# Computing the output of nine of 32 heads with 512-column matmuls and a DRAM scratch, in a decode attention kernel with gradients

## Chip, cores, metric

The kernel runs on one core of a Trainium2 chip. The metric is device time in microseconds, lower is better. Every run named here was in the fast state. A ratio between two kernels is the mean time of one's fast runs over the mean of the other's fast runs of the same rounds, so it is not quite the ratio of the medians that are quoted beside it. In the profile PE is TensorE's matmul side and PEld its weight loads, DVE is VectorE, ACT ScalarE, POOL GpSimd, and SPq the queue of SyncE, which issues the transfers. L205 is a line of the kernel of that run. Where a figure comes from the records of a trace and not from a view of the profile, the text says so.

## The reference

One query row per head, 32 heads, 8192 keys, head dimension 128, bf16. It returns the attention output and its gradients with respect to q, k and v.

```python
def _fwd_reference(q, k, v):
    scale = q.shape[-1] ** -0.5
    scores = jnp.einsum('bhqd,bhkd->bhqk', q, k) * scale
    attn = _softmax(scores, axis=-1)
    return jnp.einsum('bhqk,bhkd->bhqd', attn, v)
# reference: out, vjp = jax.vjp(_fwd_reference, q, k, v); returns out and vjp(grad_out)
```

Per head: p = softmax(q.K scale), o = p.V, dp = V.do, ds = p (dp - sum(p dp)) scale, dq = ds.K, dK = outer(ds, q), dV = outer(p, do). K and V of a head are 2.1 MB each and are read once. dK and dV are as large and are written once.

## The kernel before

A head's V lies in SBUF as 128 rows of 64 slots of 128 values. V has two buffers, so the load for head h+2 waits until head h has let go. The output o comes from 64 matmuls, each with a whole 128x128 block of V as weights and a single moving column. The sum of p dp is found as do.o, with one more matmul.

```python
    def contract(Xt, rep, out_col, first=0, last=NT):
        for n in range(first, last):
            nc.tensor.matmul(out_col, lhsT=Xt[:, n, :], rhs=rep[:, n, 0:1],
                             start=(n == 0), stop=(n == NT - 1), skip_group_check=True)
    # ... cut ...
    for h in range(H + 1):
        p_ = h - 1
        if h < H:
            x = st[h] = {}
            rows_bc(h)                 # q and do rows to all partitions, into the bank x["s"]
            for u in range(NCH):
                k_blocks(h, u)         # VectorE transposes of K, four a head
            k_scores(h)                # PE: scores
        if h > 0:
            ds_of(p_)                  # needs sum(p dp) in x["m"][:, 1:2]
            outer(p_, "dk", 0)
            dq_of(p_, 0)
        # ... cut: softmax, more of dk and dq, K load ...
        v_copy(h, 0)
        v_transposes(h, 1)
        v_transposes(h, 2)
        contract(Vt[h], x["p"], x["m"][:, 2:3])
        nc.scalar.copy(o_all[:, h:h + 1], x["m"][:, 2:3])
        v_scores(h, 0)                 # PE: dp
        v_scores(h, 1)
        v_transposes(h, 3)
        nc.tensor.matmul(x["m"][:, 1:2], lhsT=do_f[:, h:h + 1].to_broadcast([P, P]), rhs=o_all[:, h:h + 1],
                         start=True, stop=True, skip_group_check=True)
        v_scores(h, 2)
        v_scores(h, 3)
        outer(h, "dv", 0)              # VectorE; the fourth one issues the store of dv
        outer(h, "dv", 1)
        outer(h, "dv", 2)
        if 0 < h and h + 2 < H:
            load_v(h + 2)
        outer(h, "dv", 3)
```

## Time and profile before

| | before |
|---|---|
| time, median of 3 | 645.52 us (645.49 to 646.38) |
| profiled span, mean granted TensorE clock | 644.6 us, 0.601 |
| busy: PE, DVE, ACT | 482.0, 505.9, 180.7 us |
| HBM bytes | 134.23 MB read, 134.23 MB written |

The page's own lines are shown in the prediction. One plain head in order of time is needed as well, because the change inserts work there. The columns are start, length, engine, line, operation, tiles, count, and in brackets what an idle engine had waited for.

```profile
317.68 0.51 ACT L309 ACTIVATE p_rep<-e,rinv 128x256 bf16<-128x256 f32 x1 [1.98 <-DVE rinv L307]
320.07 4.63 DVE L215 TENSOR_TENSOR G_dv<-p_rep,qd 128x2048 bf16<-128x2048 bf16 x4 [2.13 <-DMA out_dram<-G_dv]
320.90 1.82 PE L205 MATMUL m_ps<-p_rep,Vt 128*128 128x1 bf16 x64
...
324.49 0.34 SPq L78 DMA_DIRECT2D Vt<-in_v_dram  x1
324.84 4.62 DVE L146 STREAM_TRANSPOSE XK_sb<-Kt 128x1024 f32<-128x1024 f32 x4
...
325.62 0.58 PE L200 MATMUL dp_ps<-do_blk,XT_sb 128*128 128x2 bf16 x16 [0.64 <-ACT XT_sb L179]
```

p is ready at 318.19. DVE does not start dv until 320.07, because the buffer of dv is still being stored. The 64 one-column matmuls take 1.82 us in all. dp is complete at 326.20, and at 328.30 three of the four K transpositions are done.

### The profile page before, as it was taken

The page shows a single profiled execution, that of the slowest core. Times are in us where ns is not written, and L with a number is a line of the kernel's source. Part 1 is how long each engine was busy: PE and PEld are TensorE (multiplying, and loading weights), DVE is VectorE, ACT ScalarE, POOL GpSimd, SP SyncE. Part 2 cuts the span into 40 slices and gives each one's busy share as a digit, 9 for nine tenths or more (in the row PEclk, how much of TensorE's full clock was granted, in tenths as well). Part 3 has the DMA queues.
Part 4 walks back from the last instruction along what each step waited for, and adds up shares of the span by engine and source line. Part 5 has one row for each costly group of instructions (what it writes and reads, how often), then busy time and mean ns, then how long its engine had stood idle before and what let it go on. Part 6 is the DMA issues. An engine that isn't in the chain of part 4 may idle for free.

```text
span 644.6 us, 20935 instructions
## 1 busy us (share of the span) xinstructions
PE 482.0 (75%) x9673; PEld 443.9 (69%) x9673; DVE 505.9 (78%) x653; ACT 180.7 (28%) x332; POOL 0.7 (0%) x6
## 2 busy tenths in 40 slices
PE   3998898886777877768776787677876777877780
PEld 2887788785676766768666687567776676866670
DVE  5999899767977679867788777787767986778761
ACT  2333333322233231333222332123322233231230
POOL 0000000000000000000000000000000000000000
PEclk9666666665566655666556665566665566655665
DMA  8999999999999999999999999999999999999985
GB/s 350 404 428 429 424 427 424 428 429 421 418 429 428 428 425 430 430 426 431 425 428 428 430 426 428 428 428 427 427 429 431 424 432 424 430 426 429 427 362 244
DMA packets 19718, 269.80 MB, mean 419 GB/s; under 512 B 2352, under 2 KB 2352, under 8 KB 2864
## 3 DMA queue, kind: packets, MB, share of 16 engines
q1 hardware_dynamic: 19584, 268.47, 98.2%
q8 instruction: 75, 1.23, 0.7%
q14 instruction: 11, 0.09, 0.0%
q10 hardware_dynamic: 48, 0.01, 0.0%
HBM read 134.23 MB, written 134.23 MB: 416 GB/s over the span
## 4 chain that ended last, share of the span: by engine, by line
DMA 62%; PE 24%; DVE 9%; ACT 1%; issue 1%; SPq 0%; DVEq 0%; ACTq 0%
DMA Vt<-in_v_dram 61%; PE T_ps L188 15%; DVE XK_sb L146 4%; DVE G_dv L215 4%; PE m_ps L205 3%; PE dp_ps L200 2%; PE s_ps L157 2%; PE dp_ps L205 1%; DVE G_dk L215 1%; DMA Kt<-in_k_dram 1%; PE m_ps L300 1%; ACT p_rep L309 0%; PE s_ps L173 0%; ACT XT_sb L179 0%; PE m_ps L288 0%
## 5 line engine op out<-in xcount | busy, mean ns | idle before, releaser
L188 PE MATMUL T_ps<-ident_f,Vt 128*128 128x128 f32 x1024 | 217.0, 383 | 27.3 <-DMA Vt<-in_v_dram 24.7
L188 PEld LDWEIGHTS T_ps<-ident_f,Vt 128*128 128x128 f32 x1024 | 182.2, 206 | 45.2 <-PE m_ps L288 21.7
L215 DVE TENSOR_TENSOR G_dv<-p_rep,qd 128x2048 bf16<-128x2048 bf16 x128 | 148.2, 1220 | 60.9 <-DMA out_dram<-G_dv 52.8
L215 DVE TENSOR_TENSOR G_dk<-ds_rep,qd 128x2048 bf16<-128x2048 bf16 x128 | 155.6, 1218 | 4.6 <-DMA out_dram<-G_dk 3.6
L146 DVE STREAM_TRANSPOSE XK_sb<-Kt 128x1024 f32<-128x1024 f32 x128 | 148.3, 1214 | 5.8 <-DMA Kt<-in_k_dram 3.2
L179 ACT COPY XT_sb<-T_ps 128x1024 f32<-128x1024 f32 x128 | 128.7, 1008 | 83.9 <-PE T_ps L188 77.2
L157 PE MATMUL s_ps<-q_blk,XK_sb 128*128 128x4 bf16 x2048 | 59.8, 168 | 94.6 <-DVE pdt L239 87.6
L157 PEld LDWEIGHTS <-XK_sb 128*128 128x128 bf16 x2048 | 57.1, 104 | 103.9 <-DVE pdt L239 96.6
L200 PE MATMUL dp_ps<-do_blk,XT_sb 128*128 128x2 bf16 x2048 | 67.0, 164 | 18.0 <-ACT XT_sb L179 17.6
L200 PEld LDWEIGHTS <-XT_sb 128*128 128x128 bf16 x2048 | 65.5, 103 | 20.7 <-ACT XT_sb L179 20.2
L205 PE MATMUL dp_ps<-ds_rep,Kt 128*128 128x1 bf16 x2048 | 64.0, 165 | 0.4 <-DVE ds_rep L241 0.4
L205 PEld LDWEIGHTS <-Kt 128*128 128x128 bf16 x2048 | 59.5, 104 | 5.7 <-issue 5.6
L249 ACT COPY dq_all<-dp_ps 128x1 f32<-128x1 f32 x32 | 5.1, 159 | 205.2 <-PE dp_ps L205 182.8
L205 PEld LDWEIGHTS <-Vt 128*128 128x128 bf16 x2048 | 57.0, 96 | 0.7
L205 PE MATMUL m_ps<-p_rep,Vt 128*128 128x1 bf16 x2048 | 56.5, 163 | 0.0
L309 ACT ACTIVATE p_rep<-e,rinv 128x256 bf16<-128x256 f32 x32 | 16.3, 508 | 64.6 <-DVE rinv L307 64.6
L307 DVE RECIPROCAL rinv<-m_ps 128x1 f32<-128x1 f32 x32 | 5.4, 168 | 35.2 <-PE m_ps L300 35.1
L234 ACT CAST qd<-s_ps 128x256 bf16<-128x256 f32 x32 | 11.9, 372 | 32.5 <-PE s_ps L230 32.5
L299 ACT ACTIVATE e<-s_ps,nbias 128x64 f32<-128x64 f32 x32 | 10.1, 314 | 32.5 <-DVE nbias L295 32.5
L241 DVE SCALAR_TENSOR_TENSOR ds_rep<-dp_ps,pdt,p_s 128x256 bf16<-128x256 f32 x32 | 15.5, 484 | 4.6 <-PE dp_ps L200 1.3
L163 DVE TENSOR_TENSOR sm<-s_ps,in_quad 128x256 f32<-128x256 f32 x32 | 13.6, 425 | 6.0 <-PE s_ps L157 2.0
L300 PEld LDWEIGHTS m_ps<-rs,ones_f 128*128 128x128 f32 x64 | 17.6, 334 | 0.0
(44 smaller groups left out, 153.1 us busy)
## 6 DMA issues: line engine op xcount, KB each, us to landing
Vt<-in_v_dram SPq DMA_DIRECT2D x32, 2048.0 KB, 30.1
Kt<-in_k_dram SPq DMA_DIRECT2D x31, 2048.0 KB, 30.3
out_dram<-G_dv SPq DMA_DIRECT2D x30, 2048.0 KB, 34.5
out_dram<-G_dk SPq DMA_DIRECT2D x30, 2048.0 KB, 33.7
out_dram<-G_dv SPq DMA_DIRECT2D x4, 1024.0 KB, 14.4
out_dram<-G_dk SPq DMA_DIRECT2D x4, 1024.0 KB, 13.2
Kt<-in_k_dram SPq DMA_DIRECT2D x4, 512.0 KB, 5.1
out_dram<-fin_sb SPq DMA_DIRECT2D x2, 8.0 KB, 12.8
```

Of the source, the lines that this page charges most:

```text
L146: nc.vector.transpose(XK[h][:, :, :, u, :], slots(Kt[h], u, NCH).rearrange("p g d -> p (g d)").bitcast(F32).rearrange("p (g w j) -> p g w ...
L157: nc.tensor.matmul(out[:, g, :], lhsT=cols[:, g, c // 2, c % 2], rhs=q_blk[:, h, c, :], start=(c == 0), stop=(c == 2 * NB - 1), skip_group ...
L163: nc.vector.tensor_tensor(x["sm"][:], x["s"][:, 0:NT].rearrange("p (a g) -> p a g", a=NQ).unsqueeze(2) .to_broadcast([P, NQ, NCH, CH]), in ...
L179: nc.scalar.copy(X[:], st[h].pop("T")[:])
L188: nc.tensor.transpose(T_ps[:, i, :], words[:, m * P:(m + 1) * P], ident_f[:])
L200: nc.tensor.matmul(st[h]["dp"][:, n:n + 2], lhsT=X[:, i, e2, :], rhs=do_blk[:, h, e2, :], start=(e2 == 0), stop=(e2 == 1), skip_group_chec ...
L205: nc.tensor.matmul(out_col, lhsT=Xt[:, n, :], rhs=rep[:, n, 0:1], start=(n == 0), stop=(n == NT - 1), skip_group_check=True)
L215: nc.vector.tensor_tensor(slots(G, r, 4).rearrange("p n (a b) -> p n a b", b=R), slots(rep, r, 4).unsqueeze(2).to_broadcast([P, Q, D // R, ...
L234: nc.scalar.copy(x["qd"][:].rearrange("p a d -> p (a d)"), x["s"][:, 256:512])
L241: nc.vector.scalar_tensor_tensor(out=x["ds"][:], in0=x["dp"][:, 0:NT].unsqueeze(2).to_broadcast([P, NT, R]), scalar=pdt[:], in1=x["p_s"][: ...
L300: nc.tensor.matmul(x["m"][:, 0:1], lhsT=ones_f[:], rhs=rs[:], start=True, stop=True, skip_group_check=True)
L309: nc.scalar.activation(x["p"][:], e[:].unsqueeze(2).to_broadcast([P, NT, R]), ACT.Copy, scale=rinv[:])
```

## The change

The intent is to spend fewer instructions on o. In nine heads (2, 5, ..., 26) four columns of p become the weights and 512 columns of V stream past them. That makes 16 matmuls in place of 64, and their result is a 4x512 array whose four diagonal 128-wide blocks sum to o. Taking a diagonal across partitions is done by a DRAM scratch: each wide head writes its array, and one strided read near the end fetches the blocks of all nine heads. As o of such a head is only known at the end, VectorE computes the sum of p dp directly, and a matmul with a matrix of ones spreads it.

```diff
+WIDE = tuple(range(2, 28, 3))
+    def o_wide(h, first, last):
+        x = st[h]
+        for g in range(first, last):
+            nc.tensor.matmul(x["s"][0:R, :], lhsT=x["p"][:, R * g:R * (g + 1), 0],
+                             rhs=Vt[h][:, R * g:R * (g + 1), :].rearrange("p n d -> p (n d)"),
+                             start=(g == 0), stop=(g == NT // R - 1), skip_group_check=True)
+        if last == NT // R:
+            four = small.tile([R, R * D], F32, tag="four", name="four")
+            nc.scalar.copy(four[:], x["s"][0:R, :])
+            nc.sync.dma_start(scratch[WIDE.index(h), 0:R * R * D].rearrange("(a c) -> a c", a=R), four[:])
+
+    def pd_of(h):
+        # ... cut: junk and pd tiles ...
+        nc.vector.tensor_tensor_reduce(out=junk[:], in0=x["p_s"][:], in1=x["dp"][:, 0:NT], scale=1.0,
+                                       scalar=0.0, op0=ALU.mult, op1=ALU.add, accum_out=pd[:])
+        nc.tensor.matmul(x["m"][:, 1:2], lhsT=ones_s[:], rhs=pd[:], start=True, stop=True, skip_group_check=True)
             for u in range(NCH):
+                if u == NCH - 1 and p_ in WIDE:
+                    pd_of(p_)
                 k_blocks(h, u)
         v_transposes(h, 1)
+        if h in WIDE:
+            o_wide(h, 0, 8)
         v_transposes(h, 2)
-        contract(Vt[h], x["p"], x["m"][:, 2:3])
-        nc.scalar.copy(o_all[:, h:h + 1], x["m"][:, 2:3])
+        if h in WIDE:
+            o_wide(h, 8, 16)
+        else:
+            contract(Vt[h], x["p"], x["m"][:, 2:3])
+            nc.scalar.copy(o_all[:, h:h + 1], x["m"][:, 2:3])
         # ... cut: the do.o matmul only if h not in WIDE ...
+        if h == WIDE[-1] + 3:
+            nc.sync.dma_start(blocks[:], scratch[:].rearrange("h (a c) -> h a c", a=R)[:, :, 0:D])
         if h == H - 1:
+            # ... cut: sum of the blocks, transpose, nine columns of o_all ...
             result(o_all, out_0)
```

More of the change, by code (lines that the diff above doesn't have):

```diff
@@ L54 @@
     small = ctx.enter_context(tc.tile_pool(name="small", bufs=2))
+    dram = ctx.enter_context(tc.tile_pool(name="scr", bufs=1, space=bass.MemoryType.DRAM))
     psT = ctx.enter_context(tc.tile_pool(name="psT", bufs=2, space=PSUM))
@@ L136, in do_columns @@
         nc.scalar.copy(do_f[:], tp[:, 2, 0:H])
+    ones_s = consts.tile([P, P], F32)
+    nc.vector.memset(ones_s[:], 1.0 / scale)
+    scratch = dram.tile([len(WIDE), R * (R + 1) * D], F32, name="scratch")
+    blocks = consts.tile([len(WIDE), R, D], F32)
     o_all = consts.tile([P, H], F32)
@@ L206, in contract @@
                              start=(n == 0), stop=(n == NT - 1), skip_group_check=True)
+    def o_wide(h, first, last):
[9 more added lines that the diff above has]
+    def pd_of(h):
+        x = st[h]
+        junk = small.tile([P, NT], F32, tag="junk")
+        pd = small.tile([P, 1], F32, tag="pd")
+        nc.vector.tensor_tensor_reduce(out=junk[:], in0=x["p_s"][:], in1=x["dp"][:, 0:NT], scale=1.0,
+                                       scalar=0.0, op0=ALU.mult, op1=ALU.add, accum_out=pd[:])
+        nc.tensor.matmul(x["m"][:, 1:2], lhsT=ones_s[:], rhs=pd[:], start=True, stop=True, skip_group_check=True)
     def outer(h, which, r):
@@ L319 @@
         v_transposes(h, 3)
-        nc.tensor.matmul(x["m"][:, 1:2], lhsT=do_f[:, h:h + 1].to_broadcast([P, P]), rhs=o_all[:, h:h + 1],
-                         start=True, stop=True, skip_group_check=True)
+        if h not in WIDE:
+            nc.tensor.matmul(x["m"][:, 1:2], lhsT=do_f[:, h:h + 1].to_broadcast([P, P]), rhs=o_all[:, h:h + 1],
+                             start=True, stop=True, skip_group_check=True)
         v_scores(h, 2)
@@ L331 @@
             load_v(2)
+        if h == WIDE[-1] + 3:
+            nc.sync.dma_start(blocks[:], scratch[:].rearrange("h (a c) -> h a c", a=R)[:, :, 0:D])
         if h == H - 1:
+            block_sum = consts.tile([len(WIDE), D], F32)
+            nc.vector.reduce_sum(block_sum[:], blocks[:].rearrange("h a d -> h d a"), axis=AX.X)
+            turned = psT.tile([P, CH // 2, P], F32, tag="T", name="turned")
+            nc.tensor.transpose(turned[:, 0, 0:len(WIDE)], block_sum[:], ident_f[0:len(WIDE), 0:len(WIDE)])
+            nc.scalar.copy(o_all[:, WIDE[0]:WIDE[-1] + 1:WIDE[1] - WIDE[0]], turned[:, 0, 0:len(WIDE)])
             result(o_all, out_0)
```

## The prediction

The text is as it was recorded, with cuts marked where it told of the hardware what no trace or run of this case shows. Cut from its sum are the terms for the 16 wide matmuls of a head: they came to 4.5 us, five at a granted clock of 0.50 ("cold" in what is left) and eleven at 1.00, with 3.5 us (all at 1.00) and 6.8 us (all at 0.50) as limits. Less the 1.77 us removed this makes the +2.7 us (+1.7 to +5.0). No such matmul is in the trace before, so these were my estimates and not shown; the trace after has since given 215 to 216 ns from start to start at 1.00 and up to 427 at 0.50, 3.5 and 6.8 us for sixteen. The forecast came to 646.0 us: nothing in the middle, about 0.5 us of transfers and tail on the 645.5. That a few engines may carry a scratch write was a guess too. In the records of the changed kernel each such write is four packets of 2 KB, with four completions 11 to 21 us after the issue (and a fifth record 0.4 us after it, before the packets), where a V load has sixteen completions.

> **What bounds the kernel now.** I read the page's slices first, because they say which resource never rests:
>
> ```profile
> PE   3998898886777877768776787677876777877780
> PEld 2887788785676766768666687567776676866670
> DVE  5999899767977679867788777787767986778761
> ...
> DMA  8999999999999999999999999999999999999985
> ```
>
> No compute engine is full in more than a few slices; the DMA row is at 9 in all but three slices, at both ends. The windows view (columns: stretch, length, busy time and instruction count of PE, PEld, DVE, ACT, POOL, then granted clock, DMA share, GB/s) sharpens this:
>
> ```profile
> 200.00:300.00 100.00, 75.34 (x1512) 69.19 (x1511) 78.63 (x100) 27.54 (x51) 0.00 (x0) 0.59 1.01 427
> 300.00:400.00 100.00, 76.67 (x1518) 70.73 (x1517) 79.41 (x101) 28.43 (x51) 0.00 (x0) 0.59 1.01 428
> ```
>
> The DMA share is 1.01 and the rate 427 to 428 GB/s from 40 to 600 us; PE and DVE rest a quarter and a fifth of the time. The bytes cannot shrink: 134.23 MB read and 134.23 MB written make 268.46 MB, and 268.46 MB / 427.5 GB/s = 628 us. The other 17 us are the start and the end (the last two slices move 362 and 244 GB/s).
>
> The chain of waits looks different at first:
>
> ```profile
> DMA 62%; PE 24%; DVE 9%; ACT 1%; issue 1%; SPq 0%; DVEq 0%; ACTq 0%
> DMA Vt<-in_v_dram 61%; PE T_ps L188 15%; DVE XK_sb L146 4%; DVE G_dv L215 4%; PE m_ps L205 3%; PE dp_ps L200 2%; PE s_ps L157 2%; PE dp_ps L205 1%; DVE G_dk L215 1%; DMA Kt<-in_k_dram 1%; PE m_ps L300 1%; ACT p_rep L309 0%; PE s_ps L173 0%;
> ```
>
> It alternates a V load with the PE work that frees that V buffer, so it would seem that a longer contraction on PE lengthens the chain. The chain in order of time shows why I don't believe this:
>
> ```profile
> 264.52 31.12 DMA Vt<-in_v_dram
> ...
> 304.93 29.59 DMA Vt<-in_v_dram
> ```
>
> A V load is 2.1 MB, 4.9 us of the full rate, yet takes 29.6 to 31.1 us from issue to landing: about 25 us of it is standing behind other transfers. And the load issued later (40.41 us after the other) landed 38.89 us after it: the late issue was taken out of the standing time. The issue list says the same of all four streams (30.1, 30.3, 34.5 and 33.7 us). A head's four 2.1 MB transfers are 8.39 MB, 19.6 us at 427.5 GB/s; the head period in the timeline is 19.4 to 20 us. **The bound is the shared transfer rate, behind a queue some six transfers deep.**
>
> [...]
>
> **The change part by part**, for each of nine wide heads (2, 5, ..., 26).
>
> ```profile
> L205 PE MATMUL m_ps<-p_rep,Vt 128*128 128x1 bf16 x2048 | 56.5, 163 | 0.0
> L320 PE MATMUL m_ps<-o_all,do_f 128*128 128x1 f32 x64 | 12.6, 266 | 0.0
> L316 ACT COPY o_all<-m_ps 128x1 f32<-128x1 f32 x32 | 5.1, 159 | 18.6 <-PE m_ps L205 18.6
> L311 DVE TENSOR_SCALAR p_s<-e,rinv 128x64 f32<-128x64 f32 x32 | 8.2, 255 | 3.4
> ```
>
> These rows are for all 32 heads. Removed: 64 one-column matmuls, busy 56.5/32 = 1.77 us (a 163 ns row, but pipelined); the o copy, 0.16 us; the fp32 product do.o, 12.6/32 = 0.4 us.
>
> Added on PE: 16 matmuls of 512 columns. [...] In the timeline of a plain head the clock is 0.50 until about 321.3 us, with p ready at 318.2 and the second group of transposes done at 319.1, then 1.00 until about 324.5. [...] So **PE gets longer, not shorter**: 3.5 to 6.8 minus 1.8, or +1.7 to +5.0 us per wide head, my choice +2.7; nine heads +15 to +45 us of 482 busy. Moving fewer instructions does not pay: the 64 small ones already stream at 28 ns each.
>
> On DVE: the product-and-sum of 128x64, about the 255 ns of the p_s row, nine times 2.3 us of 506. Its fp32 all-ones matmul replaces the do.o one, 0.4 us. On ACT: a 4x512 copy; from 256 columns in 372 ns and 1024 in 1008, (1008-372)/768 = 0.83 ns a column, 0.58 us, +0.4 us on an engine that is 28% busy.
>
> Transfers: nine writes of 8 KB and one read of 18 KB, 92 KB, 0.2 us at full rate; as each write has only four rows, a few engines may carry them, so allow 1 us. Each write stands in SP's order before the next V load, which waits for later PE work (fourth transpose group) anyway; it blocks nothing new. The read, at the end of head 29 (near 584 us), stands behind a store that takes some 34 us, so it should land near 618 to 620; its sum is wanted near 624. It and its transposition fit beside a 1.34 us DVE idle stretch there, before the last dk work.
>
> Where does the +2.7 us go? Two places. (a) V is freed later by it, so the V load, and the dv store behind it, are issued later; 25 us of standing time absorb that: no change of landing. (b) The new sum needs the last dp scores and stands on DVE before the fourth K transposition of the next head. In the plain head shown by the timeline the K transpositions start at 324.8, three end at 328.3, and dp is done at 326.2; with +2.3 to +2.7 us dp is done near 328.8, so DVE waits 0.5, works 0.3, and the scores start about 1 us late (4 us late if all matmuls are cold). But DVE has slack:
>
> ```profile
> DVE G_dv L215 <- DMA out_dram<-G_dv: 50.7, 23, 3.6
> ```
>
> From 100 to 600 us (25 heads) DVE waited 50.7 us for stores to leave, 2 us a head, 6 us per wide head with its two plain neighbours. That exceeds 1 to 4 us, so compute catches up before the queue is any thinner than some 20 us. Sum on the path: 0 in the middle, 0.2 to 1 us of transfers and tail. **646.0 us.**
>
> **The rivals.** (1) *The V chain is the bound*: each wide head then puts +2.7 (1.7 to 5.0) us into every second link of a chain of even heads (the V load of h+2 waits for h), so of nine wide heads the chain that ends last would carry four or five: about 4.5 x 2.7 = 12 us, 658 us, up to 668. For it: the chain view, 24% PE. Against: the shrinking load time and DMA share 1.01. (2) *Compute becomes the bound*: all matmuls cold and DVE's waits not recoverable, 9 x (1 to 4) = 9 to 36 us, 655 to 681. For it: DVE 78% busy, PE waits for DVE; against: the 2 us a head that DVE itself waits for stores. (3) *It gains*: the wide form is quicker or helps the clock. Even if PE gained 1.8 us per wide head, the transfers would still need 628 us plus the ends: nothing. (4) *The scratch disturbs*: the read lands late and holds DVE in head 31, or slow small transfers unbalance the engines; 1 to 5 us, 647 to 651. The margin of 4 us speaks against it.
>
> **Range and chances.** The executions before lie in 645.49 to 646.38. Below, only noise: 644.5. Above, rival 4 or a little of 2: 648.5. Faster by over 2% needs fewer bytes or a higher rate, 0.01. Slower by over 2% (above 658.4) needs rival 1 or 2 in full, 0.03. Within 2%, 0.96.
>
> **What would show it.** Right: DMA share still 1.01 and some 427 GB/s in the middle; the 16 wide matmuls of a head taking 3.5 to 6.8 us, PE busy near 482 + 24 = 506; V loads issued 2 to 5 us later in wide heads and their time to landing shorter by as much; DVE's wait for dv stores smaller than before; the small score matmuls after a wide head starting about 1 us late. Wrong: a DMA share below 1 in the heads after wide ones, V landing intervals above 40 us, or DVE waiting for the block read near the end.

## The result, and the profile after

| | before | after |
|---|---|---|
| time, median of 4 | 645.53 us (645.49 to 646.38) | 646.53 us (646.36 to 646.68) |
| ratio to before | | 1.0012, 95% interval 0.9995 to 1.003 |
| profiled span, granted clock | 644.6 us, 0.601 | 644.6 us, 0.648 |
| busy: PE, DVE, ACT | 482.0, 505.9, 180.7 us | 495.5, 508.7, 184.3 us |
| instructions | 20935 | 20121 |

The time is the same within the noise. In the page after, two rows of the slices and one row of the costliest groups answer to the rows shown before:

```profile
PE   3998888886777977788777788877787787877780
...
DMA  8999999999999999999999999999999999999995
...
L218 PE MATMUL s_ps<-Vt,p_rep 128*4 128x512 bf16 x144 | 36.4, 398 | 0.0
```

The groups with shapes kept apart show the parts that the page left out:

```profile
L223 ACT COPY four<-s_ps 4x512 f32<-4x512 f32 x9 | 5.2, 576 | 7.3 <-PE s_ps L218 7.3
...
L230 DVE CUSTOM_DVE_ANT_0 junk<-p_s,dp_ps 128x64 f32<-128x64 f32 x9 | 1.7, 190 | 2.3 <-PE dp_ps L206 2.3
...
L230 DVE DVE_READ_ACCUMULATOR2_ANT pd<- 128x1 f32 x9 | 0.7, 83 | 0.0
```

A wide head's 16 matmuls are busy 36.4/9 = 4.04 us, against 1.77 us for the 64 that they replace. Fewer instructions took longer. The mean of 398 ns in the row is the length of one matmul, which overlaps the next, not the spacing. From start to start the records show 215 to 216 ns where the granted clock was 1.00, and up to 427 ns where it was 0.50.

The windows view from 300 to 400 us (columns as in the prediction) shows the transfers exactly as full as before:

```profile
300.00:400.00 100.00, 77.42 (x1465) 67.46 (x1464) 79.82 (x104) 28.11 (x50) 0.00 (x0) 0.62 1.01 428
```

Now wide head 17 in order of time, the counterpart of the plain head above:

```profile
336.87 0.51 ACT L337 ACTIVATE p_rep<-e,rinv 128x256 bf16<-128x256 f32 x1 [2.18 <-DVE rinv L335]
...
338.16 1.89 PE L218 MATMUL s_ps<-Vt,p_rep 128*4 128x512 bf16 x8
339.37 4.63 DVE L241 TENSOR_TENSOR G_dv<-p_rep,qd 128x2048 bf16<-128x2048 bf16 x4 [2.24 <-ACT XT_sb L185]
...
341.01 1.89 PE L218 MATMUL s_ps<-Vt,p_rep 128*4 128x512 bf16 x8
...
344.18 3.50 DVE L152 STREAM_TRANSPOSE XK_sb<-Kt 128x1024 f32<-128x1024 f32 x3 [0.17 <-DMA Kt<-in_k_dram]
...
345.87 0.55 PE L206 MATMUL dp_ps<-do_blk,XT_sb 128*128 128x2 bf16 x16 [0.78 <-ACT XT_sb L185]
...
347.60 0.18 DVE L230 CUSTOM_DVE_ANT_0 junk<-p_s,dp_ps 128x64 f32<-128x64 f32 x1
```

From p ready to dp complete takes 346.42 - 337.38 = 9.0 us here, against 326.20 - 318.19 = 8.0 us in the plain head. dp is still 1.26 us earlier than the end of the third K transposition (347.68), so the new sum on DVE waits for nothing. Head 17 is one of the shorter ones: by the records of all nine wide heads the time from p to dp is 8.8 to 10.0 us, 9.4 on average, against 7.9 in the plain heads of this run. Seven of the nine have the third K transposition at 10.3 us after p, so dp is in time. In the first two, heads 2 and 5, dv was not held up by a store; there it ends 8.1 us after p, and the sum waits 1.2 and 1.1 us (the 2.3 us of the row above).

The wait printed beside dv names a copy on ACT that ended at 339.28. The records show that the store which frees the buffer of dv landed at 339.28 too, and from head 6 on every dv of this run starts 0.09 us after such a landing. So it is the same 2 us wait for a store as in the plain head, and the label of the row is not to be trusted. All the idle time of DVE before dv is the better measure, whatever it is put down to:

```profile
L215 DVE TENSOR_TENSOR G_dv<-p_rep,qd 128x2048 bf16<-128x2048 bf16 x128 | 148.2, 1220 | 60.9 <-DMA out_dram<-G_dv 52.8 <-ACT XT_sb L179 6.8 <-ACT p_rep L309 1.4
...
L241 DVE TENSOR_TENSOR G_dv<-p_rep,qd 128x2048 bf16<-128x2048 bf16 x128 | 148.2, 1220 | 58.8 <-DMA out_dram<-G_dv 48.2 <-ACT XT_sb L185 9.0 <-ACT p_rep L337 1.6
```

It is 60.9 us before and 58.8 us after: nearly the same.

The chain in order of time shows the V load after this wide head, issued at 344.75, next to the one before it on the chain:

```profile
303.97 30.30 DMA Vt<-in_v_dram
...
344.75 29.17 DMA Vt<-in_v_dram
```

It was issued 40.78 us after the other and landed 39.65 us after it. A pair like this differs by as much in the kernel before (40.41 and 38.89 us in the prediction), so the records of all V loads are the better witness. After the seven wide heads from 8 to 26 a V load is issued 20.7 to 22.2 us after the V load before it, and lands 19.8 us after that one landed, as after plain heads (19.8 to 20.5 us). From issue to landing it takes 28.9 us on average, against 30.5 us after plain heads: the late issue was taken out of the standing time.

### The profile page after: what moved, and what is told of

Same layout as the page of the kernel before. It is cut to its first block, busy times and chain, and to the rows that moved or that the text cites. A ratio compares the mean times of both kernels' runs of the same rounds, so it can differ in the third digit from the quotient of the medians.

```text
span 644.6 us, 20121 instructions
## 1 busy us (share of the span) xinstructions
PE 495.5 (77%) x9242; PEld 432.6 (67%) x9242; DVE 508.7 (79%) x673; ACT 184.3 (29%) x333; POOL 0.7 (0%) x6
## 4 chain that ended last, share of the span: by engine, by line
DMA 61%; PE 27%; DVE 7%; ACT 1%; issue 1%; SPq 0%; DVEq 0%; ACTq 0%
DMA Vt<-in_v_dram 60%; PE T_ps L194 15%; DVE XK_sb L152 3%; DVE G_dv L241 3%; PE s_ps L218 3%; PE m_ps L211 2%; PE dp_ps L206 2%; PE s_ps L163 2%; PE dp_ps L211 1%; DMA Kt<-in_k_dram 1%; PE m_ps L328 1%; DVE G_dk L241 1%; ACT XT_sb L185 0%; ACT p_rep L337 0%; PE s_ps L179 0%
## 5 line engine op out<-in xcount | busy, mean ns | idle before, releaser
L194 PE MATMUL T_ps<-ident_f,Vt 128*128 128x128 f32 x1024 | 209.5, 373 | 26.1 <-DMA Vt<-in_v_dram 24.4
L194 PEld LDWEIGHTS T_ps<-ident_f,Vt 128*128 128x128 f32 x1024 | 176.1, 201 | 44.8 <-PE m_ps L316 26.7
L241 DVE TENSOR_TENSOR G_dv<-p_rep,qd 128x2048 bf16<-128x2048 bf16 x128 | 148.2, 1220 | 58.8 <-DMA out_dram<-G_dv 48.2
L206 PEld LDWEIGHTS <-XT_sb 128*128 128x128 bf16 x2048 | 63.7, 101 | 26.4 <-ACT XT_sb L185 22.4
L211 PEld LDWEIGHTS <-Vt 128*128 128x128 bf16 x1472 | 41.3, 97 | 0.6
L211 PE MATMUL m_ps<-p_rep,Vt 128*128 128x1 bf16 x1472 | 40.8, 164 | 0.0
L218 PE MATMUL s_ps<-Vt,p_rep 128*4 128x512 bf16 x144 | 36.4, 398 | 0.0
L218 PEld LDWEIGHTS <-p_rep 128*4 128x4 bf16 x144 | 11.2, 87 | 20.1 <-issue 6.0
L260 ACT CAST qd<-s_ps 128x256 bf16<-128x256 f32 x32 | 11.9, 372 | 31.0 <-PE s_ps L256 31.0
L169 DVE TENSOR_TENSOR sm<-s_ps,in_quad 128x256 f32<-128x256 f32 x32 | 13.6, 425 | 6.5 <-PE s_ps L163 3.6
```

Source lines behind the costliest of these rows:

```text
L169: nc.vector.tensor_tensor(x["sm"][:], x["s"][:, 0:NT].rearrange("p (a g) -> p a g", a=NQ).unsqueeze(2) .to_broadcast([P, NQ, NCH, CH]), in ...
L194: nc.tensor.transpose(T_ps[:, i, :], words[:, m * P:(m + 1) * P], ident_f[:])
L206: nc.tensor.matmul(st[h]["dp"][:, n:n + 2], lhsT=X[:, i, e2, :], rhs=do_blk[:, h, e2, :], start=(e2 == 0), stop=(e2 == 1), skip_group_chec ...
L218: nc.tensor.matmul(x["s"][0:R, :], lhsT=x["p"][:, R * g:R * (g + 1), 0], rhs=Vt[h][:, R * g:R * (g + 1), :].rearrange("p n d -> p (n d)"), ...
L241: nc.vector.tensor_tensor(slots(G, r, 4).rearrange("p n (a b) -> p n a b", b=R), slots(rep, r, 4).unsqueeze(2).to_broadcast([P, Q, D // R, ...
L260: nc.scalar.copy(x["qd"][:].rearrange("p a d -> p (a d)"), x["s"][:, 256:512])
```

## The experiments

Twelve kernels ran, in four calls of three. All expectations were on record before the run.

### Twice and four times the wide matmuls

```diff
+            for _ in range(1):        # 3 in wide_x4
+                nc.tensor.matmul(x["m"][0:R, :], lhsT=x["p"][:, R * g:R * (g + 1), 0],
+                                 rhs=Vt[h][:, R * g:R * (g + 1), :].rearrange("p n d -> p (n d)"),
+                                 start=True, stop=True, skip_group_check=True)
```

The copies go to a bank that is free at that time. Results stay correct. The question is whether PE time in the V chain becomes kernel time (rival 1). The expectation puts 230 ns on a copy, an estimate: in the changed kernel's trace the matmuls start 215 to 216 ns apart at a granted clock of 1.00, and take 4.04/16 = 252 ns on average.

> Every wide product is done a second time into another bank, so each of the nine wide heads has 16 more matmuls of 512 columns, about 16 x 230 ns = 3.7 us more on PE before V is freed and before dp is ready. Theory (the transfers are the bound and their queue absorbs late V loads; DVE's waits for stores absorb late dp): 645.5 to 648 us, DMA share about 1.01 in the middle, V loads to landing shorter by some 3 to 4 us after wide heads. Rival (the chain V load, PE work, V load is the bound): about half of the nine wide heads lie on that chain, 4.5 x 3.7 = 17 us more, about 663 us.

Measured: 649.76 us (649.22 to 650.02), ratio to before 1.0058 (1.0043 to 1.0073). This is 3.2 us over the changed kernel's 646.5, and 1.8 us above the upper edge of what the theory expected. It is far from the 663 us of rival 1. From 300 to 400 us the transfers are as full as ever. From 100 to 200 us they are not quite: 423 GB/s in place of the 428 of the changed kernel, about 1.2 us of transfers (an estimate from these two rates).

```profile
100.00:200.00 100.00, 89.11 (x1536) 74.91 (x1534) 83.70 (x113) 29.71 (x55) 0.00 (x0) 0.69 1.01 423
...
300.00:400.00 100.00, 82.66 (x1490) 71.48 (x1488) 79.51 (x105) 29.28 (x52) 0.00 (x0) 0.64 1.01 427
```

The waits view (engine and line that waited, for what, us in total, times, longest) shows who paid:

```profile
DVE G_dv L245 <- DMA out_dram<-G_dv: 38.4, 20, 2.3
...
DVE junk L234 <- PE dp_ps L206: 30.4, 9, 5.0
```

DVE now waits 30.4/9 = 3.4 us per wide head for dp, and all its idle time before dv falls by 16 us:

```profile
L245 DVE TENSOR_TENSOR G_dv<-p_rep,qd 128x2048 bf16<-128x2048 bf16 x128 | 148.2, 1221 | 42.6 <-DMA out_dram<-G_dv 38.4
```

Against the changed kernel, 28 us of new waits for dp cost 3 us of time.

> Three further copies of every wide product: 48 more matmuls, about 11 us more PE in each of nine wide heads. Theory: dp is some 11 us late, the head in hand has about 1 us of margin, and DVE's waits for stores give some 2.2 us in each of three heads, 6.6 us; so about 3.5 us per wide head can't be regained, 9 x 3.5 = 32 us, if the queue (about 25 us of standing time) does not carry part of it; 655 to 680 us, with a DMA share below 1.01 in the middle. Rival (V chain is the bound): 4.5 x 11 = 50 us, about 696 us.

Measured: 673.83 us (673.27 to 675.11), ratio 1.0435 (1.0419 to 1.0451), inside what the theory expected and 22 us below the rival. Here the reserve is used up:

```profile
300.00:400.00 100.00, 93.60 (x1350) 69.63 (x1348) 70.44 (x93) 27.21 (x46) 0.00 (x0) 0.74 0.97 398
```

```profile
DVE junk L234 <- PE dp_ps L206: 106.7, 9, 13.0
...
DVE G_dv L245 <- DMA out_dram<-G_dv: 1.3, 1, 1.3
```

The waits for dp come to 106.7 us, 11.9 us per wide head. DVE's waits for stores are gone (1.3 us; its idle time before dv is 9.7 us in all), and the transfers run at 398 GB/s. The time grew by 27 us over the changed kernel. So the reserve is real and finite: about 5 us of DVE waiting per three heads (58.8 - 9.7 us over nine wide heads), plus a queue.

### 27 wide heads

```diff
-WIDE = tuple(range(2, 28, 3))
+WIDE = tuple(range(0, 27))
```

> Heads 0 to 26 wide, 27 in place of nine. Theory: each wide head puts 2.3 us more on PE and 0.26 us more on DVE, within that head's own margin (about 1 us before DVE stalls for dp, and 2 us of DVE waits for stores), so no loss: 645.5 to 649 us, PE busy about 520 us, DMA share 1.01. Rival (V chain): 13.5 x 2.3 = 31 us more than before, about 676 us. Rival (compute becomes the bound when no plain head follows to catch up): DVE waits for stores gone, 650 to 665 us.

Measured: 649.25 us (649.07 to 650.85), ratio 1.0051 (1.0034 to 1.0067). The V chain rival's 676 us is out again. PE is busy 528.9 us and the transfers stay at 428 GB/s from 100 to 600 us. DVE still waits 49.0 us for stores, so compute had not become the bound either. Yet the time is 2.7 us above the changed kernel, slightly over what the theory expected. Where those microseconds come from is taken up under the drift of the engines below.

### A quarter of the stores: the change without the transfers over it

```diff
+            L = NT // parts
+            nc.sync.dma_start(rows_of(dst, h, c, parts)[:, 0:L // 4, :], G[:, c * L:c * L + L // 4, :])
-            nc.sync.dma_start(rows_of(dst, h, c, parts), slots(G, c, parts))
```

dk and dv are incomplete on purpose, so these runs are counted as wrong. All arithmetic is still done. What is left is a kernel whose time is set by compute.

> The kernel before with only a quarter of each dk and dv store sent (outputs wrong on purpose): 134 + 34 = 168 MB, 168 / 427.5 GB/s = 393 us of transfers, so the transfers are no longer the bound. Theory: a plain head's own work is its 19.4 us period less 2.1 us of DVE waiting for a store and 0.8 us of PE waiting for V, 16.6 us; 32 x 16.6 + some 15 us of ends = 546 us (535 to 565). If instead the V chain or compute were the bound of the full kernel, the time would stay near 645 us.

Measured: 562.49 us (561.19 to 563.10), within the range. Removing only bytes took 83 us off. In this kernel DVE is the fullest engine (92%), and the transfers run at 310 GB/s in place of 428:

```profile
200.00:300.00 100.00, 85.75 (x1736) 79.84 (x1733) 91.69 (x118) 33.16 (x60) 0.00 (x0) 0.62 0.89 310
```

> The changed kernel with a quarter of the stores (outputs wrong on purpose). This shows what the change costs in compute when no queue hides it. Theory: PE gets 2.3 us longer per wide head and dp is then about 1 us late for DVE, which also does 0.26 us more: 9 x 1.3 = 12 us over the quartered kernel before (3 to 25 us). Rival (the wide form really saves time that the transfers hide): 5 to 15 us under it.

Measured: 570.37 us (568.16 to 574.20). Over the quartered kernel before that is 7.9 us of medians, 0.883/0.8705 = 1.014 of the ratios. So the change costs compute time. The waits view names the place:

```profile
DVE junk L230 <- PE dp_ps L206: 14.3, 9, 3.4
```

All nine sums now wait for dp, 1.6 us each. In the full kernel only those of heads 2 and 5 did, 2.3 us together. The difference is that in the other seven DVE has itself been held up 2 us by the store of dv.

> Quarter of the stores, o of all heads by the old 64 one-column matmuls, but the sum p*dp by VectorE in the nine heads: the second part of the change alone (outputs wrong on purpose). Theory: 9 x 0.26 us = 2.4 us over the quartered kernel before (0 to 5 us); the rest of the difference of the changed kernel belongs to the wide matmuls.

Measured: 564.11 us (559.02 to 565.53), 1.6 us over the quartered kernel before. The runs scatter by more than that, and the two intervals overlap (0.8677 to 0.8761 against 0.8688 to 0.8722), so the cost of the sum alone can't be told from nothing. Most of the 7.9 us belongs to the wide matmuls and what comes with them, the copy, the scratch and the sum of the blocks, which this run leaves out too.

### The scratch transfers, and the microsecond between the medians

> The changed kernel again, in the same rounds as the two below, for a tighter interval: 645.5 to 647 us, ratio to before 1.000 to 1.002.

Measured: 646.49 us (646.40 to 646.61) against 646.07 us for before (645.77 to 647.02), ratio 1.0004 (0.9992 to 1.0017).

```diff
-            nc.sync.dma_start(scratch[...], four[:])
-            nc.sync.dma_start(blocks[:], scratch[...])
+    nc.vector.memset(blocks[:], 0.0)
```

> The changed kernel without its nine scratch writes and the read (o of the wide heads is wrong on purpose). If the about 1 us between the kernels comes from the small transfers, which only a few engines carry, this is back at 645.5 us; if it comes from the compute or the tail, it stays at 646.5 us.

Measured: 646.28 us (646.13 to 646.45), ratio to before 1.0001 (0.9988 to 1.0015). Its output o is wrong on purpose.

```diff
# the kernel before, plus, in the nine heads:
+            nc.scalar.copy(fr[...], x["qd"][0:R]...)
+            nc.sync.dma_start(scratch[...], fr[:])
# and at the end of head 29 the read of the blocks, in head 31 a sum of them that nothing uses
```

> The kernel before with nine such scratch writes of 4 rows of 2 KB, and the read of the blocks at the end of head 29, added and nothing else. If the small transfers cost the about 1 us: 646.5 us; otherwise 645.5 us.

Measured: 646.03 us (645.65 to 646.35), ratio 0.9996 (0.9983 to 1.0008). Both intervals contain 1, and so does that of the changed kernel. The scratch traffic costs nothing that these rounds can show. The read of the blocks landed at 617.9 us in the changed kernel, where the prediction had 618 to 620. The 1 us between the first medians shrank to 0.4 us in these rounds, and no cause can be given for it.

### The drift of the sixteen engines

What made wide_x2 and wide_27 about 3 us slower, with the transfers full or nearly so? For each of these transfers the trace records sixteen completions. I take each for the share of one of the core's 16 DMA engines. The transfer is finished with the last: in the kernel before, the last completion of the last V load came at 614.17 us, and the transpositions that wait for it start at 614.30. For V loads of the kernel before, in us after the first share (my sorting of those records, not a page of the profile):

```
issued   the sixteen shares, after the first
  4.3    0.0 0.1 0.1 0.1 0.2 0.2 0.2 0.2 0.2 0.4 0.5 0.5 0.6 0.6  0.7  2.1
225.7    0.0 0.1 0.1 0.1 0.4 0.6 3.3 4.5 5.2 5.3 6.0 6.1 6.4 6.5  6.9  7.2
583.2    0.0 0.1 0.1 0.1 0.4 1.7 6.1 12.5 13.2 13.2 13.4 13.6 13.7 13.9 14.6 16.0
```

By this reading the engines start together and drift apart; five or six keep pace, nine fall 12 to 16 us behind. For the last V load of five runs, on the span's clock:

| | first share lands | last share lands | spread | profiled span |
|---|---|---|---|---|
| before | 598.2 | 614.2 | 16.0 | 644.6 |
| after | 598.1 | 612.7 | 14.6 | 644.6 |
| after_again | 599.0 | 612.6 | 13.6 | 644.4 |
| wide_x2 | 598.9 | 616.2 | 17.3 | 648.1 |
| wide_27 | 597.5 | 617.3 | 19.8 | 649.1 (its slowest run) |

In wide_27 the first engine was even 0.6 us earlier than in the changed kernel, and the last one 4.6 us later; the span is 4.5 us longer. In wide_x2 all engines lost 0.8 us and the last one another 2.7 us. So most of these extra microseconds sit on the slowest engine. In both runs a single engine stands out (the next slowest are at 13.6 and 13.3 us). Why that one fell behind is not known.

The general drift has a suspect. The page lists a queue of kind "instruction" with 75 packets of 16 KB, about one in 8 us. (The next expectation calls them instruction fetches, a reading of the queue's name.) In the kernel before, the sum of the sixteen lags grew from 8.6 to 129.1 us while 68 of these packets went by, 1.77 us per packet; in the changed kernel it was 1.74. The other traces on record fit less well. From 40 to 600 us it was about 1.6 us per packet in after_again, 1.8 in wide_x2, and 2.0 in wide_27, where only 58 packets went by and the sum grew as much as before. In wide_x4 63 packets went by and the sum grew by only some 10 us, with the sixteen shares of most V loads within 5 us. There the transfers ran at 398 to 413 GB/s, not 428, so engines that lagged may have caught up in the pauses; that is argued, not shown. The packets are thus a suspect and no more. Two last experiments tried to use and to test this.

> The kernel before with 4950 memsets of one column on GpSimd, which is idle otherwise (about 100 ns each, 15 us of each head's 20). They touch nothing that others read. Instruction fetches went 75 for 20935 instructions, so some 18 more packets of 16 KB. In the trace the sum of the sixteen engines' lags grows by 1.7 to 1.8 us per fetch. Theory (the fetches make the engines drift apart): sum of lags 30 us larger near the end, the slowest engine 2 to 4 us later, time 648 to 650 us. Rival (the drift has another cause): same number of fetches or more, but the sum of lags and the time stay, 645.5 to 646.5 us.

```diff
     for h in range(H + 1):
         p_ = h - 1
+        for _ in range(150):
+            nc.gpsimd.memset(fill[:], 0.0)
         # ... cut: the tile fill, 128x1 f32, is made before the loop ...
```

Measured: 779.88 us (779.70 to 780.05). As a measurement of time this failed by my own mistake. A memset is 99 ns busy but they follow each other every 157 ns, so 4950 of them take 778 us and set the span themselves:

```profile
L264 POOL MEMSET fill<- 128x1 f32 x4950 | 490.8, 99 | 285.3
```

The trace of the other engines can still be read. The added instructions arrived by another queue, in 8 KB packets, 51 in place of 11:

```profile
q8 instruction: 75, 1.23, 0.6%
q14 instruction: 51, 0.41, 0.1%
```

The sum of lags grew by 143 us in place of 120 between 40 and 600 us, the spread of the last V load was 21.0 in place of 16.0 us, and the last store was issued at 635.83 in place of 630.82 us. That is the sign that the theory expected, with 23 us of lags where it had 30, and 5 us on the slowest engine where it had 2 to 4. It supports these packets as a cause of the drift. It is one run, its time is no witness, and the memsets themselves could have disturbed the transfers: no run with as many memsets and fewer such packets tells these two apart. So I call it supported, not settled.

> The kernel before, with only the last 1 MB store (second half of dk of head 31) cut into rows 0 to 123 and rows 124 to 127 in place of 128 rows. [...] the traced scratch writes show these four to be among the early ones (0.5 to 5.6 us behind the first, the late nine 11 to 16). In the kernel before, the sixteen shares of the last store land at 0.0 (six), 0.2, and 6.2 to 9.0 us. Theory (the end is set by the slowest of sixteen engines that have drifted apart): the late nine or ten lose 2.4 us of work, the four gain 7.4 us and then end together with them: 2.4 us less, 643.5 us (1 to 3 us less). Rival (the end is set by the last stores' issue or by the total of bytes): same time or up to 7 us more, as four engines carry 1 MB at some 27 GB/s each.

The cut passage said which engines a transfer of 124 or 4 rows runs on; "these four" are the four that carry the scratch writes, by the four completions of each. That 124 rows run on four engines too was not shown when this was written. The run fits it: from 640 to 642 us, with the 124 rows still under way, its DMA share is 0.25, four of sixteen.

```diff
+            if h == H - 1 and which == "dk" and c == 1:
+                for a, b in ((0, 124), (124, 128)):
+                    nc.sync.dma_start(rows_of(dst, h, c, parts)[a:b], slots(G, c, parts)[a:b])
             # ... cut: otherwise the whole store as before ...
```

Measured: 648.56 us (648.46 to 648.79), ratio 1.0036 (1.0022 to 1.005). A miss: 2.5 us slower, not 2.4 faster.

> The changed kernel with the same last store. Theory: 2.4 us less than the changed kernel, 644 us. Rival: no gain, 646.5 us or more.

Measured: 647.87 us (647.39 to 647.94), ratio 1.0024 (1.001 to 1.0037). Also a miss.

The completion records say what happened (on the span's clock). In tail4_before the shares of the store before the last ended at 631.3 to 640.4 us, where the original kernel's last 1 MB store had ended at 643.4. So the twelve others were done 3.0 us earlier, near the 2.4 us worked out. The four, though, ended at 642.8 to 645.2 with the 124 rows, and 0.3 us later with the other four. I had given them 31 packets of 309 ns (the median of the 8 KB packets in the trace before), 9.6 us from 631.3. They took 11.4 to 13.9 us; some packets of 8 KB took up to 740 ns in the last 4 us. Why is not known. The end followed the slowest engine, as the theory says, but I overloaded four of them. No version that beats both kernels came out of this study.

## Why the prediction was right

The time was predicted at 646.0 us (644.5 to 648.5) and measured at 646.53 and 646.49 us. By its steps:

- **The transfers are the bound: shown.** Cutting only stores took 83 us off, and the DMA share stayed at 1.01 and the rate at 428 GB/s after the change.
- **PE gets longer, not shorter: shown.** The matmuls took 4.04 us per wide head where 4.5 was put. The prediction had counted five at half the clock; the records show none in four of the nine heads and at most four in the others (215 to 216 ns from start to start at a granted clock of 1.00, up to 427 at 0.50). The +2.7 us that I chose is thereby +2.3 us. PE's total rose by 13.5 us, not by 24, because the transpositions of V became quicker at the same time: 209.5 us in place of 217.0, at a granted clock of 0.648 in place of 0.601.
- **DVE's sum 0.26 us, ACT's copy 0.58 us: right.** They took 190 + 83 = 273 ns and 576 ns.
- **V loads issued 2 to 5 us later, landing no later: right in kind, too large in size.** By the records the V load is issued 7.1 to 8.3 us after p in wide heads, against 6.2 in plain ones: 0.9 to 2.1 us later, and it lands no later. I had let the whole +2.7 us through. In eight of the nine wide heads the granted clock stayed at 1.00 for 10.2 us (6.8 in head 20), against 3.4 us in nearly all plain ones, and the transpositions of V beside the wide matmuls took 5.7 to 6.1 us, against about 6.8 in plain heads. That the clock would be granted longer was not in the prediction; rival 3 had only named it.
- **Scores about 1 us late: wrong in the full kernel.** From p to the scores it took 11.6 us in wide heads and 11.5 in plain ones once the stores held dv up. DVE waited for dp in two of nine heads, 2.3 us together. The margin was read rightly from the plain head, 8.0 us to dp and 10.1 to the third K transposition. What was too large is the delay put into it: 2.3 to 2.7 us where it was 1.4 on average. That it stayed inside the margin is probably owed to the clock above (no run holds the clock down to test it), so here the prediction had some luck. The margin itself comes from the stores, because DVE's wait for the dv store delays the K transpositions as well; with the stores cut, the wait for dp appears in all nine, 1.6 us each.
- **DVE's waits for stores absorb the delay: shown for the larger delays,** by the fall of its idle time before dv from 58.8 us to 42.6 in wide_x2 and to 9.7 in wide_x4. The change itself hardly drew on them (60.9 to 58.8 us): its delay fitted into the margin just named.
- **Rival 1 (the V chain): refuted** by wide_x2 (+3 us for 30 us of added PE busy time, where it asked for 17) and by wide_27. **Rival 2 (compute):** true only from about four times the work on. **Rival 3 (a hidden gain):** refuted by the quartered kernels, which show a loss of 8 us. **Rival 4 (the scratch):** not seen in either direction; so the 0.5 us that the prediction put on top for transfers and tail is not shown to be anything but noise.
- **What I did not foresee:** the end is set by the slowest of sixteen drifting engines, so the queue does not absorb everything. This is where wide_x2 and wide_27 left the theory, by 1.8 and 0.3 us.

## What to carry to other kernels

When a chain of waits consists mostly of loads that take six times their bare transfer time (here 29.6 to 31.1 us against 4.9 us at 427.5 GB/s), issue one later and see whether it lands later. If it does not, work on that chain is likely to be free, as here, until the other engines' own waits for transfers are used up. To learn what a change costs in compute under such a bound, cut the stores in both kernels and compare again. Replacing many one-column matmuls by a few wide ones does not save TensorE time as such: here 64 took 1.8 us and 16 took 4.0 us. A label of a wait is worth a check: DVE's wait for the dv store was put down to an ACT copy when the two ended at the same time (339.28 us).
